# Threshold attention and a gated MLP: thresholding on GpSimd, VectorE or ScalarE by step, and q, k transposes by half tiles

## The chip, the cores and the metric

The kernel runs on one core of a Trainium2 chip. The core has TensorE (PE: matmuls and their weight loads), VectorE (DVE), ScalarE (ACT), GpSimd (POOL) and SyncE (SP, which here issues nearly all DMAs); each has an instruction queue of its own and runs it in order, and waits on the others by semaphores. Matrix products land in PSUM, which DVE and ACT read out; everything else lies in SBUF. The metric is the device time of one execution in microseconds (us), lower is better; the time before is 428.83 us, the median of three runs (428.46 to 429.54).

## The reference

Attention over 8 batches x 8 heads, 576 positions, 64 columns a head, in float32; only scores within tau = 0.02 of a row's maximum take part. Its output, with the heads side by side, goes through a gated MLP that also mixes positions.

```python
scale = 1.0 / np.sqrt(q.shape[-1])                       # 0.125
scores = scale * np.matmul(q, k.transpose(0, 1, 3, 2))
thresh = np.max(scores, axis=-1, keepdims=True) - tau
scores = np.where(scores >= thresh, scores, -1000000000.0)
scores = scores - np.max(scores, axis=-1, keepdims=True)
attn = np.exp(scores)
attn = attn / (np.sum(attn, axis=-1, keepdims=True) + 1e-09)
x = np.matmul(attn, v)          # then (8, 576, 512)
h = np.maximum(x @ w_in, 0.0)   # 1024 columns, halves u and v
v_n = (v - mu) / np.sqrt(var + 1e-06)
v_s = np.einsum('ts,bsd->btd', w_spatial, v_n) + b_spatial[None, :, None]
out = (u * v_s) @ w_out
```

## The kernel before

**Steps.** Heads are taken in pairs, 4 pairs a batch, 32 in all. A pair's 576 rows of queries make 4.5 blocks of 128, so that two pairs make 9 steps, a batch 18 and the kernel 144. A step `g` has 128 query rows against 576 keys for two heads (h = 0, 1). It goes through these stages, each a token in a list:

- `S`, `Y` (`scores`, `scores_end`, line 830): float32 matmuls on 64x64 tiles of the PE array into one of two PSUM rings `s_ring`; heads and row halves run beside each other. Between the first part and the last part of a step lies `G`: an empty instruction on a relay engine (GpSimd, or with a prefix `a` ACT, with `v` DVE), which waits for the first part and for which the last part waits (the two heads share a bank).
- `M` (`top`, line 859): for each head one custom DVE instruction that copies the scores from PSUM to the buffer `e` (a ring of three) and gives the row maximum `peak`, two instructions a step.
- `B` (`shift`, lines 869 on DVE and 873 on GpSimd): `negm`, two numbers a row, from the maxima and tau.
- `E`, `F` (`spread`): one ACT instruction for each head, 128x576, called a half here. A table `WAYS` has a letter for each step. Way `a` (102 steps): Prelu with a slope of 1e30 for negative values (line 890), then `Z` (`exps`, line 925): Exp of both heads at once, 128x1152, to the float16 buffer `p` (a ring of ten). Way `n` (42 steps): Exp straight to float16 (line 887), then on DVE `C` (`keep`, line 909), which makes a mask of bits, and `A` (`pick`, line 918), which ands it with the exponentials as int32 to `p`.
- `T` (line 930): SP issues a DMA that transposes `p` to `pT`; three of 144 steps are transposed on PE instead (`RP`, `rp`).
- `P`, `i`, `p` (lines 505 to 548): PE multiplies `pT` with v and a column of ones, DVE divides by the sum and writes `xn`.

**q and k.** They come by DMA (`ql`, `kl`), are brought into another order on GpSimd (`sq`, line 306, to `qn` and `kn`), and are transposed on PE in float32 by `qk_main`: `QA` four 128x128 transposes of q into one PSUM bank, evicted by `qa` with a factor of 0.125; `QB` and `qb` the same of k without it (lines 448, 422 to 430). The last 64 rows of both go through `QR`, `qr` (line 467), with no factor, which `B`, `E` and `F` make good. PSUM banks for all work but the scores come from a ring of two, `f_ring`.

**The MLP** of one or two batches back runs between the steps: `v` with `ev`, `bv`, `bs`, `ba`, `N` (normalization, the last on GpSimd, lines 696 to 708), `u`, `eu`, `s`, `es`, `o`, `eo`.

**Order.** No scheduler is at work. `ORDER` has a list of some 300 tokens for each of the 8 batches, and `LAST` four short ones for the end; `run_token` issues a token's instructions. A token `X7:1` is stage X of step 7 of the batch one before the list's, `:-1` of the next one. A prefix `d` moves an eviction from ACT to DVE. Each engine's queue has the order in which the tokens stand, and so a token that waits holds up all behind it on its engine.

## Time and profile before

| | before |
|---|---|
| median of 3 runs | 428.83 us (428.46 to 429.54) |
| the profiled execution | 429.39 us |
| its span, first to last instruction | 427.6 us |
| granted TensorE clock | 1.00 |
| packets of the main DMA queue, as a share of 16 engines' span | 102.3% |
| batches, from the first `M` of one to that of the next | 39.4, 48.6, 52.8, 48.3, 49.9, 51.3, 47.6, 46.7 us |
| from the last `M` to the end | 35.5 us |

Rows of the profile are read so: line, engine, operation, what it writes `<-` what it reads, shapes, `x`count, then busy us and mean ns of one; behind the second bar stands the idle time of the engine just ahead of these instructions with what ended it. Rows that a line's or tile's view prints have the shortest, the median and the longest duration in ns instead. PE is matmuls, PEld weight loads. The chain is the work that ended last, followed back from the end. Matmuls overlap and their ends are modelled, so a PE that is busy throughout may still hold small gaps.

### The profile page before, as it was taken

The page shows a single profiled execution, that of the slowest core. Times are in us where ns is not written, and L with a number is a line of the kernel's source. Part 1 is how long each engine was busy: PE and PEld are TensorE (multiplying, and loading weights), DVE is VectorE, ACT ScalarE, POOL GpSimd, SP SyncE. Part 2 cuts the span into 40 slices and gives each one's busy share as a digit, 9 for nine tenths or more (in the row PEclk, how much of TensorE's full clock was granted, in tenths as well). Part 3 has the DMA queues.
Part 4 walks back from the last instruction along what each step waited for, and adds up shares of the span by engine and source line. Part 5 has one row for each costly group of instructions (what it writes and reads, how often), then busy time and mean ns, then how long its engine had stood idle before and what let it go on. Part 6 is the DMA issues. An engine that isn't in the chain of part 4 may idle for free.

```text
span 427.6 us, 13266 instructions
## 1 busy us (share of the span) xinstructions
PE 405.0 (95%) x4978; PEld 253.3 (59%) x5029; DVE 384.0 (90%) x1035; ACT 386.1 (90%) x567; POOL 191.4 (45%) x469
## 2 busy tenths in 40 slices
PE   8778978999999999999999999999999999999995
PEld 4456655566555675575665657656665666565642
DVE  6999989999899899989999999989999989999562
ACT  4999979999999999999999999999999999999362
POOL 2566437763246633554235631374233753255020
PEclk9999999999999999999999999999999999999999
DMA  7999999999999999998999989999989999989913
GB/s 196 288 280 182 263 273 227 168 182 195 239 265 171 214 213 188 204 210 227 214 165 280 211 165 252 217 221 210 236 138 229 228 214 206 160 150 214 180 57 117
DMA packets 224703, 88.18 MB, mean 206 GB/s; under 512 B 195648, under 2 KB 220352, under 8 KB 224640
## 3 DMA queue, kind: packets, MB, share of 16 engines
q1 hardware_dynamic: 224192, 86.75, 102.3%
q8 instruction: 39, 0.64, 0.6%
q10 hardware_dynamic: 368, 0.33, 0.2%
q0 software_dynamic: 80, 0.26, 0.2%
q14 instruction: 24, 0.20, 0.2%
HBM read 32.79 MB, written 9.44 MB: 99 GB/s over the span
## 4 chain that ended last, share of the span: by engine, by line
PE 62%; DVE 11%; ACT 9%; DMA 7%; issue 5%; POOL 3%; SPq 1%; POOLq 0%; DVEq 0%; ACTq 0%
PE s L830 25%; DVE e L859 7%; PE f L752 6%; DMA pT<-p 6%; PE f L448 5%; PE f L510 5%; PE f L723 4%; PE f L656 4%; ACT e L890 3%; PE f L781 3%; ACT e L887 2%; PE f L505 2%; ACT p L925 1%; DMA xT<-xn 1%; PE f L641 1%
## 5 line engine op out<-in xcount | busy, mean ns | idle before, releaser
L859 DVE CUSTOM_DVE_ANT_0 e<-s,zero 128x576 f32<-128x576 f32 x288 | 204.3, 752 | 5.8 <-PE s L830 1.4
L830 PE MATMUL s<-qkT 64*64 64x160 f32 (+1 forms) x2304 | 172.9, 413 | 4.5 <-DVE peak L859 3.7
L890 ACT ACTIVATE e<-e,negm 128x576 f32<-128x576 f32 x204 | 148.3, 766 | 4.8 <-PE s L830 2.3
L830 PEld LDWEIGHTS s<-qkT 64*64 64x64 f32 x2304 | 105.3, 132 | 53.2 <-issue 19.1
L925 ACT ACTIVATE p<-e 128x1152 f16<-128x1152 f32 x102 | 117.1, 1157 | 0.8
L873 POOL TENSOR_SCALAR negm<-peak 128x2 f32<-128x2 f32 x93 | 21.5, 231 | 133.3 <-DVE peak L859 89.7
L887 ACT ACTIVATE e<-e,negm 128x576 f16<-128x576 f32 x84 | 62.4, 767 | 2.0 <-POOL negm L873 1.3
L510 PE MATMUL f<-v,pT 128*128 128x65 bf16 x984 | 44.6, 194 | 0.0
L510 PEld LDWEIGHTS <-pT 128*128 128x128 f16 x1024 | 41.9, 98 | 2.4 <-issue 0.6
L918 DVE TENSOR_TENSOR p<-e 128x576 int32<-128x576 int32 x42 | 34.4, 822 | 0.5
L752 PE MATMUL f<-wsT,vn 128*128 128x512 bf16 x121 | 31.9, 380 | 0.9 <-DVE qkT L424 0.2
L505 PE MATMUL f<-v,pT 128*128 128x130 bf16 x123 | 27.2, 221 | 4.0 <-DMA pT<-p 3.9
L333 POOL CAST v<-vl 128x512 bf16<-128x512 f32 x32 | 21.3, 666 | 18.6 <-PE s L830 17.5
L708 POOL TENSOR_SCALAR vn<-vrel,rs,nm 128x512 bf16<-128x512 f32 (+1 forms) x35 | 27.9, 798 | 3.6
L723 PE MATMUL f<-xT,w_in 128*128 128x512 bf16 x102 | 28.5, 380 | 1.0 <-ACT qkT L430 0.3
L656 PE MATMUL f<-w_in,xT 128*128 128x512 bf16 x98 | 27.0, 380 | 1.4 <-DMA xT<-xn 0.3
L548 DVE TENSOR_TENSOR xn<-f,r 128x384 bf16<-128x384 f32 x46 | 25.2, 554 | 0.7
L781 PE MATMUL f<-w_o,gT 128*128 128x512 bf16 x94 | 25.1, 379 | 0.4
L859 DVE DVE_READ_ACCUMULATOR2_ANT peak<- 128x1 f32 x288 | 23.9, 83 | 0.0
L306 POOL COPY qn<-ql 128x512 f32<-128x512 f32 x31 | 19.7, 636 | 5.9 <-DMA ql<-in_q_dram 2.7
L752 PEld LDWEIGHTS <-vn 128*128 128x128 bf16 x140 | 12.8, 98 | 15.5 <-issue 3.1
L448 PE MATMUL f<-identf,kn 128*128 128x128 f32 x124 | 19.8, 282 | 2.2 <-DVE qkT L424 1.5
(175 smaller groups left out, 560.2 us busy)
## 6 DMA issues: line engine op xcount, KB each, us to landing
vl<-in_v_dram SPq DMA_DIRECT2D x16, 512.0 KB, 5.2
ql<-in_q_dram SPq DMA_DIRECT2D x15, 512.0 KB, 5.5
kl<-in_k_dram SPq DMA_DIRECT2D x15, 512.0 KB, 5.7
out_dram<-oo SPq DMA_DIRECT2D x12, 512.0 KB, 4.2
pT<-p SPq DMA_TRANSPOSE x141, 4.4
uT<-in_moe_w_in_dram SPq DMA_DIRECT2D x3, 512.0 KB, 6.4
uT<-in_moe_w_spatial_dram SPq DMA_DIRECT2D x2, 576.0 KB, 6.8
vx<-in_v_dram SPq DMA_DIRECT2D x16, 64.0 KB, 3.8
```

Source lines behind the costliest of these rows:

```text
L448: nc.tensor.transpose(out=t[:, c * P:(c + 1) * P], in_=nat[i][which][:, c, :], identity=identf)
L505: nc.tensor.matmul(out=t[:, at:at + 130], lhsT=pt[:, 4, rows], rhs=vt[:, 4:6, :].rearrange("p b d -> p (b d)"), start=True, stop=False)
L510: nc.tensor.matmul(out=t[:, at + 65 * h:at + 65 * h + 65], lhsT=pt[:, 5 * h + j, rows], rhs=vt[:, 6 * h + j, :], start=False, stop=(h == 1 ...
L656: nc.tensor.matmul(out=t, lhsT=x_of(b, f, slice(c * P, (c + 1) * P)), rhs=w_in[:, f, 512:1024], start=(f == 0), stop=(f == 3))
L723: nc.tensor.matmul(out=t, lhsT=w_in[:, m, f * P:(f + 1) * P], rhs=x_of(b, m, slice(0, 512)), start=(m == 0), stop=(m == 3))
L752: nc.tensor.matmul(out=t, lhsT=vn[:, c, f * P:(f + 1) * P], rhs=wsT[:, c, 0:512], start=(c == 0), stop=(c == 4))
L781: nc.tensor.matmul(out=t[:n], lhsT=gs[b][:, f, c * P:c * P + n], rhs=w_o[:, f, :], start=(f == 0), stop=(f == 3))
L830: made.append(nc.tensor.matmul(out=s_ring[g % 2][halves[k], at[h] + lo:at[h] + hi], lhsT=qks[n][halves[h], 0, m:m + 64], rhs=qks[n][halves ...
L859: nc.vector.tensor_tensor_reduce(out=e_ring[g % 3][:, h, :], in0=view(s_ring[g % 2], at[h], [[1, S]]), in1=zero.broadcast_to([P, S]), scal ...
L887: nc.scalar.activation(out=half_e(g)[0][:, h, :], in_=s, func=ACT.Exp, bias=bias_, scale=scale if steps[g][1] == 4 else 1.0)
L890: nc.scalar.activation(out=e, in_=s, func=ACT.Prelu, bias=bias_, scale=scale if steps[g][1] == 4 else 1.0, alpha=1e30)
L925: nc.scalar.activation(out=numerators(g), in_=e_ring[g % 3].rearrange("p h s -> p (h s)"), func=ACT.Exp)
```

## The change

**The threshold.** Scores are no longer scaled through q; `M` scales them as it copies (`scale=scale` where 1.0 stood), so that `peak` is scaled too. `B` becomes `bound`: `low` = tau - peak, on GpSimd or with a prefix `d` on DVE. A half (`E`, `F`) becomes one of two things. With a prefix `a` it is a Prelu on ACT as before, then Exp with a bias of -tau. Otherwise it is a `tensor_scalar` on GpSimd, or with `d` on DVE, in place on `e`: add `low`, multiply by 2^-126. What is added lies below tau, so the product is a subnormal number; its bits read as an int32 are the difference in steps of 2^-23, or, where the difference was negative, a number near -2^31. `Z` reads them as int32 with a scale of 2^-23 and a bias of -tau; a negative difference becomes about -256 and its exponential 0. The ways `n`, the mask, the pick and the table `WAYS` go. Of 288 halves 132 are on GpSimd, 60 on DVE and 96 on ACT; `Z` is on ACT for all 144 steps. `e` gets a fourth buffer, `p` loses one of ten.

**q and k.** `QX` makes 16 transposes of 64 rows each, the upper and the lower half of every block in turn, into both PSUM banks of the ring; `qx` and `qy` evict one bank each (q and k of one half). Bringing q and k into order may be done on ACT (`ask`, `asq`), which 27 of 62 are.

**Lists.** All lists are new.

```diff
-    "S0:0 aG0:0 Y0:0 S1:0 G1:0 Y1:0 L7:0 L8:0 M0:0 B0:0 L9:0 Ci1:0 QA1:0 qa1:0 F0:0 M1:0 sk1:0 B1:0 sv0:0 "
+    "S0:0 vG0:0 Y0:0 M0:0 B0:0 ask1:0 L5:-1 S1:0 vG1:0 Y1:0 S2:0 G2:0 Y2:0 M1:0 F0:0 QX1:0 qx1:0 L7:0 L4:-1 "
...
-    e_ring = [const.tile([P, 2, S], F32, name=f"e{i}") for i in range(3)]
-    p_ring = [const.tile([P, 1152], F16, name=f"p{i}") for i in range(10)]
+    e_ring = [const.tile([P, 2, S], F32, name=f"e{i}") for i in range(NE)]
+    p_ring = [const.tile([P, 1152], F16, name=f"p{i}") for i in range(NP)]
...
-    def qk_main(i, which):
-        hold = {}
+    def qk_main(i):
+
+        hold = []
 
         def mm():
-            t = hold["t"] = bank()
-            for c in range(4):
-                nc.tensor.transpose(out=t[:, c * P:(c + 1) * P], in_=nat[i][which][:, c, :],
-                                    identity=identf)
-
-        def ev():
-            if which == 0:
-                evict(qk_of(i)[:, 0, 64:S], hold["t"], mul=scale)
-            else:
-                evict(qk_of(i)[:, 1, 64:S], hold["t"])
-        return "act", mm, ev
+            hold.extend(bank() for _ in range(2))
+            for c in range(8):
+                w, n = divmod(c, 4)
+                for r in range(2):
+                    nc.tensor.transpose(
+                        out=hold[r][:, 64 * c:64 * c + 64], in_=nat[i][w][halves[r], n, :],
+                        identity=identf[halves[r], halves[r]])
+
+        def ev(r):
+            dst = qk_of(i)[:, :, 64:S].rearrange("p w (c s) -> p w c s", c=4)
+            evict(dst[:, :, :, 64 * r:64 * r + 64],
+                  hold[r].rearrange("p (w c s) -> p w c s", w=2, c=4))
+        return "act", mm, lambda: ev(0), lambda: ev(1)
...
+    def bound(g):
+
+        low[g] = small.tile([P, 2], F32, name="low")
+        (nc.vector if on_vector[0] else nc.gpsimd).tensor_scalar(
+            out=low[g], in0=peak[g], scalar1=-1.0, scalar2=tau, op0=ALU.mult, op1=ALU.add)
+
+    def spread(g, h):
+
+        e = e_ring[g % NE][:, h, :]
+        if on_scalar[0]:
+            plain.add(g)
+            nc.scalar.activation(out=e, in_=e, func=ACT.Prelu, bias=low[g][:, h:h + 1], alpha=1e30)
         else:
...
+            (nc.vector if on_vector[0] else nc.gpsimd).tensor_scalar(
+                out=e, in0=e, scalar1=low[g][:, h:h + 1], scalar2=2.0 ** (SHIFT - 149),
+                op0=ALU.add, op1=ALU.mult)
...
+    def exps(g):
+
+        e = e_ring[g % NE].rearrange("p h s -> p (h s)")
+        if g in plain:
+            nc.scalar.activation(out=numerators(g), in_=e, func=ACT.Exp, bias=wrap)
         else:
...
+            nc.scalar.activation(out=numerators(g), in_=e.bitcast(I32), func=ACT.Exp, bias=wrap,
+                                 scale=2.0 ** -SHIFT)
```

`NE` is 4, `NP` is 9, `SHIFT` is 23 for this tau, `wrap` is -tau in every row.

How the queues move is seen at three places, all in batch 0. First PE, where pair 1's q and k are transposed between scores (`s_96`, `s_97` are the score rings, `f_91`, `f_92` the two banks, `rl` the last rows); before:

```order
L448 MATMUL f_91<-identf,qn 128x128 x4
L830 MATMUL s_96<-qkT 64x160 x2
L830 MATMUL s_96<-qkT 64x416 x4
L830 MATMUL s_96<-qkT 64x160 x2
L448 MATMUL f_92<-identf,kn 128x128 x4
L467 MATMUL f_91<-identf,rl_144 128x128
```

and now, from the last couple of the 16 transposes on:

```order
L445 MATMUL f_91<-identf,kn 128x64
L445 MATMUL f_92<-identf,kn 128x64
L815 MATMUL s_97<-qkT 64x160 x2
L815 MATMUL s_97<-qkT 64x416 x4
L815 MATMUL s_97<-qkT 64x160 x2
L464 MATMUL f_91<-identf,rl_143 128x128
```

Two groups on one bank each, with a step of scores between them, have become one group that alternates between both banks. Second ACT, early in batch 0 (`e_...` are the ring's buffers, `p_...` the numerators); before, from the first pair's evictions on:

```order
L430 COPY qkT<-f_92 128x512
L430 COPY qkT<-f_91 128x2x64
L925 ACTIVATE p_111<-e_108 128x1152
L887 ACTIVATE e_109<-e_109,negm 128x576 x2
L890 ACTIVATE e_107<-e_107,negm 128x576 x2
L887 ACTIVATE e_108<-e_108,negm 128x576
L925 ACTIVATE p_113<-e_107 128x1152
L887 ACTIVATE e_108<-e_108,negm 128x576
```

and now:

```order
L422 COPY qkT<-f_91 128x2x4x64
L875 ACTIVATE p_110<-e_106,wrap 128x1152
L859 ACTIVATE e_107<-e_107,low 128x576 x2
L875 ACTIVATE p_112<-e_108,wrap 128x1152
L422 COPY qkT<-f_92 128x2x64
L859 ACTIVATE e_106<-e_106,low 128x576 x2
L873 ACTIVATE p_111<-e_107,wrap 128x1152
L299 COPY kn<-kl_141 128x512
```

Every step had two halves on ACT; now some steps (line 875) leave it only the exponential, and copies of q and k have come. Third GpSimd at about the same place (`v`, `w_in` and `wsb` are v and weights brought to bfloat16); before:

```order
L873 TENSOR_SCALAR negm<-peak 128x2
L333 CAST v_133<-vl_140 128x2x4x64
L339 CAST v_133<-vx_146 64x64 x2
L873 TENSOR_SCALAR negm<-peak 128x2
L333 CAST v_134<-vl_143 128x2x4x64
L339 CAST v_134<-vx_146 64x64 x2
L353 CAST w_in<-uT 128x1024
```

and now:

```order
L861 TENSOR_SCALAR e_108<-e_108,low 128x576
L851 TENSOR_SCALAR low<-peak 128x2
L861 TENSOR_SCALAR e_107<-e_107,low 128x576
L346 CAST w_in<-gT 128x1024
L457 COPY qkT<-qkT 64x64
L861 TENSOR_SCALAR e_107<-e_107,low 128x576
L346 CAST w_in<-uT 128x1024
L861 TENSOR_SCALAR e_106<-e_106,low 128x576
```

The halves stand between the bounds, the casts of the weights and the copies of the first rows (`qkT<-qkT`), and what follows a half in this queue starts after it.

More of the change, by code (lines that the diff above doesn't have):

```diff
@@ L13 @@
 I32 = mybir.dt.int32
-U16 = mybir.dt.uint16
 AX = mybir.AxisListType
@@ L434 @@
     rest_late = (0, 1, 2)
+    halves = [slice(64 * k, 64 * k + 64) for k in range(2)]
     def qk_of(i):
@@ L494, in first @@
         turn(tq, 0, 0, 0)
-        nc.scalar.mul(out=qkt[:, 0, 64:192], in_=tq[:, 0:P], mul=scale)
+        nc.scalar.copy(out=qkt[:, 0, 64:192], in_=tq[:, 0:P])
         for c in range(1, 4):
             turn(tm, P * (c - 1), 0, c)
-        nc.scalar.mul(out=qkt[:, 0, 192:576], in_=tm[:, 0:384], mul=scale)
-    halves = [slice(64 * k, 64 * k + 64) for k in range(2)]
+        nc.scalar.copy(out=qkt[:, 0, 192:576], in_=tm[:, 0:384])
     def weigh(t, at, pt, vt, rows=slice(0, P)):
@@ L850, in scores_end, with top @@
         follow(part(g, 1, 0, S - cut)[0], turned[g])
-    negm, peak = {}, {}
-    def top(g, heads=slice(0, 2)):
-        if g not in peak:
-            peak[g] = small.tile([P, 2], F32, name="peak")
-        for h in range(heads.start, heads.stop):
+    peak, low, plain = {}, {}, set()
+    def top(g):
+        peak[g] = small.tile([P, 2], F32, name="peak")
+        for h in range(2):
             nc.vector.tensor_tensor_reduce(
-                out=e_ring[g % 3][:, h, :], in0=view(s_ring[g % 2], at[h], [[1, S]]),
-                in1=zero.broadcast_to([P, S]), scale=1.0, scalar=float("-inf"),
+                out=e_ring[g % NE][:, h, :], in0=view(s_ring[g % 2], at[h], [[1, S]]),
+                in1=zero.broadcast_to([P, S]), scale=scale, scalar=float("-inf"),
@@ L862, in top @@
                 op0=ALU.add, op1=ALU.max, accum_out=peak[g][:, h:h + 1])
-    def shift(g, engine):
-        nm = negm[g] = small.tile([P, 2], F32, name="negm")
-        down = -(scale if steps[g][1] == 4 else 1.0)
-        if engine is nc.vector:
-            engine.scalar_tensor_tensor(out=nm, in0=peak[g], scalar=down,
-                                        in1=raised[:, 0 if way(g) == "a" else 1, :],
-                                        op0=ALU.mult, op1=ALU.add)
-        else:
-            engine.tensor_scalar(out=nm, in0=peak[g], scalar1=down,
-                                 scalar2=float(tau) + (0.0 if way(g) == "a" else half_step),
-                                 op0=ALU.mult, op1=ALU.add)
@@ L877, in half_e @@
-    def half_e(g):
-        t = e_ring[g % 3].bitcast(F16)
-        return t[:, :, 0:S], t[:, :, S:2 * S]
-    def spread(g, h):
-        s = e_ring[g % 3][:, h, :]
-        e, bias_ = e_ring[g % 3][:, h, :], negm[g][:, h:h + 1]
-        if way(g) in "nrs":
-            nc.scalar.activation(out=half_e(g)[0][:, h, :], in_=s, func=ACT.Exp,
-                                 bias=bias_, scale=scale if steps[g][1] == 4 else 1.0)
-        elif on_act(g):
-            nc.scalar.activation(out=e, in_=s, func=ACT.Prelu, bias=bias_,
-                                 scale=scale if steps[g][1] == 4 else 1.0, alpha=1e30)
-        else:
-            nc.scalar.activation(out=e, in_=s, func=ACT.Exp, bias=bias_)
@@ L1123, in run_token @@
         kind = name.rstrip("0123456789")
-        a = [int(x) for x in name[len(kind):]] if kind not in "SGYMHKBEFZWCAT" else []
-        g = 18 * b + int(name[len(kind):]) if kind in "SGYMHKBEFZWCAT" else 0
+        a = [int(x) for x in name[len(kind):]] if kind not in "SGYMBEFZT" else []
+        g = 18 * b + int(name[len(kind):]) if kind in "SGYMBEFZT" else 0
         if b >= B or g >= len(steps):
-            return
-        if kind in stepwise and way(g) not in stepwise[kind]:
             return
@@ L1185 @@
         nc.vector.memset(zero, 0.0)
-        nc.gpsimd.memset(raised[:, 0], float(tau))
-        nc.gpsimd.memset(raised[:, 1], float(tau) + half_step)
-        nc.vector.memset(ntau, -float(tau))
+        nc.vector.memset(wrap, -float(tau))
         nc.vector.memset(mhalf, -0.5)
-        nc.scalar.activation(out=ctau, in_=ntau, func=ACT.Exp)
+        nc.scalar.activation(out=used, in_=wrap, func=ACT.Exp)
         nc.vector.tensor_copy(out=identb, in_=identf)
```

94 lines of the change are left out of this document (30 added, 64 removed), and 279 rows, old and new, of tables (LAST, ORDER).

## The prediction

> **What bounds the kernel now.** I read the page first, busy shares and then the chain that ended last, and after it the same quantities cut at the batch borders.
>
> ```profile
> PE 405.0 (95%) x4978; PEld 253.3 (59%) x5029; DVE 384.0 (90%) x1035; ACT 386.1 (90%) x567; POOL 191.4 (45%) x469
> ...
> PE 62%; DVE 11%; ACT 9%; DMA 7%; issue 5%; POOL 3%; SPq 1%; POOLq 0%; DVEq 0%; ACTq 0%
> ```
>
> Three engines are at 90% or more and GpSimd is at 45%; the chain is mostly PE, yet over a third of it is not. An average cannot say where that third lies. The borders of the next view are the starts of the first maxima (line 859) of batches 0, 1 and 2, and the end of the last one. Columns: the stretch, its length, then busy time (and instructions) of PE, weight loads, DVE, ACT and POOL.
>
> ```profile
> 7.50:46.90 39.40, 33.29 (x449) 22.29 (x442) 38.66 (x105) 37.02 (x53) 22.21 (x53) 1.00 1.15 257
> 46.90:95.50 48.60, 44.17 (x580) 27.14 (x584) 45.49 (x123) 44.28 (x66) 29.56 (x69) 1.00 1.10 216
> 95.50:392.10 296.60, 291.41 (x3610) 183.65 (x3649) 276.95 (x739) 284.97 (x414) 133.52 (x329) 1.00 1.08 208
> 392.10:427.60 35.50, 30.08 (x312) 16.89 (x314) 18.86 (x49) 17.20 (x32) 4.53 (x9) 1.00 0.55 131
> ```
>
> Batch 0 is bound by DVE (38.66 of 39.40 us) with ACT just behind, and PE idles 6.1 us. In batch 1 all three are within 1.4 us of each other and PE idles 4.4 us. Batches 2 to 7 are PE's: 291.4 of 296.6 us, 5.2 us idle. The tail is the last batch's second half, which has hardly any threshold work. The chain, asked for separately in the first 88 us and in the 297 us after them, agrees:
>
> ```profile
> by line: DVE e L859 17.5%; PE s L830 11.9%; issue 10.9%; ACT e L890 7.0%; DMA pT<-p 6.6%; ACT e L887 6.5%; ACT p L925 4.4%; POOL v L333 3.3%; PE f L723 3.2%; PE f L510 2.9%; POOL v L339 2.5%; DVE p L918 2.4%; POOL w_in L353 1.9%; PE f L448
> ...
> by line: PE s L830 32.4%; PE f L752 8.2%; PE f L448 7.1%; PE f L510 5.8%; PE f L656 5.1%; PE f L723 4.7%; DMA pT<-p 4.6%; PE f L781 4.5%; DVE e L859 4.3%; issue 3.7%; ACT e L890 2.5%; PE f L505 2.0%; DMA xT<-xn 1.7%; ACT e L887 1.2%; PE f L
> ```
>
> So what the change does for ACT and DVE can pay in the first two batches, and from batch 2 on only through PE's own work. Line 448, the q and k transposes that the change rewrites, is 7.1% of the second stretch's chain.
>
> **The threshold: what each engine loses and gets.** The prices stand in these rows.
>
> ```profile
> L890 ACT ACTIVATE e<-e,negm 128x576 f32<-128x576 f32 x204 | 148.3, 766 | 4.8 <-PE s L830 2.3
> L925 ACT ACTIVATE p<-e 128x1152 f16<-128x1152 f32 x102 | 117.1, 1157 | 0.8
> L887 ACT ACTIVATE e<-e,negm 128x576 f16<-128x576 f32 x84 | 62.4, 767 | 2.0 <-POOL negm L873 1.3
> L918 DVE TENSOR_TENSOR p<-e 128x576 int32<-128x576 int32 x42 | 34.4, 822 | 0.5
> L909 DVE TENSOR_SCALAR e<-e 128x1152 uint16<-128x1152 f16 x42 | 19.8, 474 | 1.3 <-ACT e L887 0.9
> L306 POOL COPY qn<-ql 128x512 f32<-128x512 f32 x31 | 19.7, 636 | 5.9 <-DMA ql<-in_q_dram 2.7 <-PE s L830 1.9
> ...
> L428 ACT ACTIVATE qkT<-f 128x512 f32<-128x512 f32 x18 | 10.6, 589 | 3.4 <-PE f L448 3.4
> L869 DVE SCALAR_TENSOR_TENSOR negm<-peak,raised 128x2 f32<-128x2 f32 x51 | 10.3, 202 | 1.3 <-PE s L830 0.6
> ```
>
> ACT loses 148.3 + 62.4 + 117.1 = 327.8 us. It gets 96 Prelu halves at 0.766 (73.5), 144 exponentials over both heads at 1.157 (166.6; 96 of them read the bits as int32, for which no ACT row exists: I price them like the float32 ones, the nearest row, between nothing and a doubling of 1.157) and 27 q and k copies taken from GpSimd, at 0.589 (15.9). That is 386 - 328 + 256 = 314 us.
>
> DVE loses mask and pick, 34.4 + 19.8, and 51 shifts, 10.3. It gets 56 bounds of two numbers (0.2 each, 11) and 60 threshold halves, a form that the trace lacks. Bounds for a half are the plain float32 copy and the two-scalar operation below, stretched from 512 to 576 columns: 0.48 and 0.62 us. I take 0.55, so 33 us. DVE comes to about 384 - 65 + 44 = 363.
>
> GpSimd gets 132 halves and gives up 27 copies of 0.636 (17). The nearest row is its own two-operation TENSOR_SCALAR, 0.767 for 512 columns against 0.192 for 2: 1.13 ns a column, so 0.84 us for 576. From below the copy's 0.610 gives 0.66; from above a doubling, 1.68, which is what a held copy shows (1.204 against 0.610). I take 0.84: 111 us, and POOL comes to 191 + 111 - 17 = 285.
>
> ```profile
> L321 DVE COPY kn<-kl x1: 427/427/427, 3.4 to 3.4; 128x512 f32<-128x512 f32 x1
> L970 DVE TENSOR_SCALAR vn<-vrel,rstd,shift x2: 547/742/936, 412.4 to 413.1; 128x512 bf16<-128x512 f32 x2
> L970 POOL TENSOR_SCALAR vn<-vrel,rstd,shift x1: 768/768/768, 413.0 to 413.0; 128x512 bf16<-128x512 f32 x1
> L708 POOL TENSOR_SCALAR vn<-vrel,rs,nm x35: 761/767/1202, 77.3 to 389.4; 128x512 bf16<-128x512 f32 x28, 64x512 bf16<-64x512 f32 x7
> L873 POOL TENSOR_SCALAR negm<-peak x93: 190/192/719, 9.0 to 393.0; 128x2 f32<-128x2 f32 x93
> L306 POOL COPY kn<-kl x31: 606/610/1204, 9.3 to 358.2; 128x512 f32<-128x512 f32 x31
> L918 DVE TENSOR_TENSOR p<-e x42: 725/758/1476, 12.1 to 395.7; 128x576 int32<-128x576 int32 x42
> ```
>
> These rows also show DVE and GpSimd holding each other up: the same DVE operation takes 547 ns, and 936 when GpSimd's 768 ns one starts just before it; the pick doubles from 758 to 1476, GpSimd's copy from 610 to 1204. [...] What the rows make of it: GpSimd busy 285 of 428 us is two thirds, so about 40 of the 60 DVE halves wait half of 0.84, 17 us on DVE; in return the 84 masks and picks, which do the same now, are gone. DVE ends at 380 at worst, no more than today, so the sum stands without it; it feeds the second rival.
>
> Behind a GpSimd half queue now the bounds, the casts of v and 46 of the 144 relay nops for which PE's last score part waits (68 before; 98 are on ACT and DVE instead of 76). A nop behind a half is late by up to 0.84 us. What covers this is that PE has other work placed between a step's first and last score parts; a fourth e buffer gives every step one more step of time. Each is worth nothing if the cover holds. If a third of the 46 were late by 0.4 it would cost 6 us, and that end stays in the range. One p buffer fewer is covered by the transposes' count and order, which stay at 141 on SP's queue.
>
> **First two batches.** Batch 0 (list 0 puts 15 halves on GpSimd, 10 on ACT, 7 on DVE): DVE loses 7 masks and picks, 7 x 1.296 = 9.1, and gets 7 x 0.55 = 3.9, so 38.66 becomes 33.5, level with PE's 33.3. Batch 1 (21, 6, 9): DVE 45.5 - 5 x 1.296 + 9 x 0.55 = 44.0; POOL 29.6 - 6 x 0.636 + 21 x 0.84 = 43.4; PE 44.2. PE's idle 10.5 us is then the most there is to win. **Batches 2 to 7**: at most PE's 5.2 us. Of the 15.7 us together I take two thirds, 10.5, because GpSimd, loading DMAs and the issue gaps of the chain remain.
>
> **q and k by half tiles.** Before, two groups of four 128x128 transposes a pair; now one group of 16 on 64 rows each, two halves beside each other.
>
> ```profile
> 163.22 0.60 PE L448 MATMUL f<-identf,qn 128*128 128x128 f32 x4
> ...
> L448 PE MATMUL f<-identf,qn 128*128 128x128 f32 x124 | 19.8, 282 | 0.1
> ...
> 209.10 0.48 PEld L830 LDWEIGHTS s<-qkT 64*64 64x64 f32 x16 [0.27 <-issue]
> L830 PEld LDWEIGHTS s<-qkT x2304: 129/133/133, 6.1 to 390.2; 64*64 64x64 f32 x192
> ```
>
> Four transposes take 0.60 us with one at 0.28, so they follow each other every 0.11 us: 8 x 0.11 = 0.87 us a pair. The score rows, the only ones on 64-row tiles, show four tiles loading at once (16 loads of 0.133 in 0.48 us). Two halves should thus run side by side; the streamed columns halve, from 128 to 64, but each half still loads 128 weight columns. If the streamed columns decide, a couple takes 0.055 us and the group 0.44; if the loads decide, 0.11 and 0.87, as now; if halves don't overlap, 16 x 0.11 = 1.74. I take 0.87, no change, because the couple's load is as wide as today's and today's pace of 0.11 would be reached by either. [...] The group needs both f banks at once, so later users of these banks wait for both evictions, 0.59 (ACT) or 0.69 (DVE); scores stand behind nearly every group, and a step of them is over 1 us.
>
> **Sum.** The profiled execution took 429.39 us, 1.8 us more than its span, and the median is 428.83. 429.4 - 10.5 + 0 = 418.9, and 0.6 less against the median: **418 us**.
>
> **Rivals.** (1) *Half tiles at the pace of their streamed columns*: 31 groups save 0.43 us, 24 of them where PE is the bound, 10.3 us: 408. For it: line 448's 7.1% of the chain, and that loads overlap on 64-row tiles. Against it: the width of the load. [...] (2) *GpSimd becomes the pace*, the slower side. Its place is batches 0 and 1, where GpSimd also shapes v and the weights. In batch 1 it holds 25.7 us besides 21 halves, so it decides from (48.6 - 25.7) / 21 = 1.09 us a half. At a mean of 1.4 batch 1 takes 25.7 + 29.4 = 55 us and batch 0 (four copies fewer) 22.2 - 2.5 + 21.0 = 40.7, together 7.7 us more, with nothing won later: 437. For it: held GpSimd operations double, and subnormal results have no row. Against it: most DVE work, the maxima of line 859, holds nothing up. (3) *Halves in series*: 24 x 0.87 = 21 us more, 439. (4) *Waits change places*: SP's transposes (DMA is 7% of the chain, unchanged in number) and late relays eat what is won: 428.5.
>
> **Chances.** Forecast 0.46, (1) 0.24, (2) 0.12, (3) 0.06, (4) 0.12. The forecast's own range is 413 to 424, from all of the 15.7 us to a third of it. The whole range, 404 to 433, takes in (1) and (4) and leaves out (3), most of (2) and the far end of (1), under 0.2. A difference of 0.3% is about what can be told from no change, so faster means under 427.5 and slower over 430.1. Faster: 0.46 + 0.24 + 0.05 of (4) = 0.75; same: 0.07; slower: 0.18.
>
> **What would show it.** Right: batch 0 near 35 us with no engine over 95%; PE still at 98% from batch 2 on; ACT near 315 to 325 in all, POOL near 285, a GpSimd half at 0.8 to 0.9. First rival: a group of 16 lasting 0.6 us or less from first start to last end, and fewer busy PE us in the long stretch. Second: GpSimd halves over 1.1 us on average and DVE or ACT waiting for POOL in the first 95 us. Wrong altogether: PE under 95% busy in batches 2 to 7 with waits for relays or for f banks at its head.

## The result and the profile after

| | before | after |
|---|---|---|
| median of 20 runs each, side by side | 430.25 us (427.26 to 433.24) | 428.61 us (423.57 to 434.78) |
| ratio | | 0.9935, 95% interval 0.9906 to 0.9964 |
| the profiled execution, its span | 429.39, 427.6 us | 428.80, 426.9 us |
| granted TensorE clock of it | 1.000 | 0.991 |
| batches 0 and 1; 2 to 7; the rest, from the profile | 88.0; 296.6; 43.0 us | 88.0; 295.6; 43.3 us |

The change makes the kernel faster by 0.65%, a quarter of the 2.5% that were forecast; on the 428.83 us from which the prediction counts, that is 426.0. The ratio is below that of the medians because it leaves disturbed runs out, five of the 20 of the changed kernel, each over 1.5% above its fastest. A second comparison (the unaltered kernel among the experiments) gave 0.9902 (0.9873 to 0.9931).

The page of the changed kernel, its busy shares and its chain, against the two lines that the prediction began with:

```profile
PE 398.4 (93%) x5230; PEld 248.3 (58%) x5277; DVE 363.0 (85%) x1001; ACT 342.4 (80%) x459; POOL 265.6 (62%) x567
...
PE 71%; DVE 14%; DMA 5%; issue 4%; ACT 3%; SPq 1%; POOL 1%; DVEq 0%; ACTq 0%; POOLq 0%
```

ACT fell from 90% to 80% and DVE from 90% to 85%, as meant, and GpSimd rose from 45% to 62%. No engine but PE is near its limit, yet the span is the same. The stretches between the same borders (length, then busy time of PE, weight loads, DVE, ACT and POOL, the granted clock, the share of the DMA engines, GB/s):

```profile
8.10:47.20 39.10, 31.28 (x446) 20.45 (x439) 34.76 (x95) 31.74 (x40) 29.15 (x58) 0.96 1.15 255
47.20:96.10 48.90, 44.55 (x634) 29.34 (x637) 43.26 (x119) 41.43 (x56) 35.66 (x74) 0.97 1.11 217
96.10:391.70 295.60, 285.65 (x3814) 177.78 (x3846) 262.71 (x718) 249.46 (x329) 194.02 (x421) 1.00 1.06 209
391.70:426.90 35.20, 30.21 (x313) 16.92 (x314) 18.22 (x50) 17.12 (x30) 5.28 (x8) 0.98 0.52 127
```

Three things stand here. In batch 0 DVE has 3.9 us less to do and ACT 5.3 less, and the batch is 0.3 us shorter. In the long stretch PE has 5.8 us less to do, and 1.0 arrives. And the clock, 1.00 in every stretch before, is 0.96 and 0.97 in the first two.

The groups of the page that carry the new prices (busy us, mean ns of one; behind the bar the engine's idle time just ahead):

```profile
L843 DVE CUSTOM_DVE_ANT_0 e<-s,zero 128x576 f32<-128x576 f32 x288 | 203.9, 751 | 17.4 <-PE s L815 14.9
...
L875 ACT ACTIVATE p<-e,wrap 128x1152 f16<-128x1152 int32 x96 | 119.3, 1252 | 7.1 <-POOL e L861 3.3
L861 POOL TENSOR_SCALAR e<-e,low 128x576 f32<-128x576 f32 x132 | 100.2, 759 | 35.9 <-DVE low L851 15.1
L859 ACT ACTIVATE e<-e,low 128x576 f32<-128x576 f32 x96 | 70.5, 767 | 8.3 <-DVE low L851 3.4
L873 ACT ACTIVATE p<-e,wrap 128x1152 f16<-128x1152 f32 x48 | 59.7, 1253 | 1.5 <-PE s L815 0.6
...
L861 DVE TENSOR_SCALAR e<-e,low 128x576 f32<-128x576 f32 x60 | 36.5, 624 | 1.1 <-POOL low L851 0.8
```

and the maxima in the kernel before:

```profile
L859 DVE CUSTOM_DVE_ANT_0 e<-s,zero 128x576 f32<-128x576 f32 x288 | 204.3, 752 | 5.8 <-PE s L830 1.4
```

A GpSimd half takes 0.759 us (0.84 forecast), a DVE half 0.624 (0.55), an exponential 1.25 where 1.157 was forecast, whether it reads float32 or int32. The maxima show where much of DVE's relief of 21 us went: they now wait 14.9 us for PE's scores, where they waited 1.4 us before.

### The profile page after: what moved, and what is told of

The parts are those of the page before. It is cut to its first block, busy times and chain, and to the rows that moved or that the text cites. A ratio compares the mean times of both kernels' runs of the same rounds, so it can differ in the third digit from the quotient of the medians.

```text
span 426.9 us, 13687 instructions
## 1 busy us (share of the span) xinstructions
PE 398.4 (93%) x5230; PEld 248.3 (58%) x5277; DVE 363.0 (85%) x1001; ACT 342.4 (80%) x459; POOL 265.6 (62%) x567
## 4 chain that ended last, share of the span: by engine, by line
PE 71%; DVE 14%; DMA 5%; issue 4%; ACT 3%; SPq 1%; POOL 1%; DVEq 0%; ACTq 0%; POOLq 0%
PE s L815 30%; DVE e L843 8%; PE f L747 7%; PE f L651 5%; PE f L718 5%; PE f L505 5%; PE f L445 4%; DMA pT<-p 3%; PE f L776 3%; DVE e L861 2%; PE f L500 2%; PE f L636 1%; PE f L464 1%; DMA kl<-in_k_dram 1%; DVE qkT L416 1%
## 5 line engine op out<-in xcount | busy, mean ns | idle before, releaser
L843 DVE CUSTOM_DVE_ANT_0 e<-s,zero 128x576 f32<-128x576 f32 x288 | 203.9, 751 | 17.4 <-PE s L815 14.9
L815 PE MATMUL s<-qkT 64*64 64x160 f32 (+1 forms) x2304 | 176.7, 417 | 8.2 <-DVE peak L843 7.1
L875 ACT ACTIVATE p<-e,wrap 128x1152 f16<-128x1152 int32 x96 | 119.3, 1252 | 7.1 <-POOL e L861 3.3
L861 POOL TENSOR_SCALAR e<-e,low 128x576 f32<-128x576 f32 x132 | 100.2, 759 | 35.9 <-DVE low L851 15.1
L859 ACT ACTIVATE e<-e,low 128x576 f32<-128x576 f32 x96 | 70.5, 767 | 8.3 <-DVE low L851 3.4
L873 ACT ACTIVATE p<-e,wrap 128x1152 f16<-128x1152 f32 x48 | 59.7, 1253 | 1.5 <-PE s L815 0.6
L851 POOL TENSOR_SCALAR low<-peak 128x2 f32<-128x2 f32 x88 | 18.6, 211 | 53.5 <-DVE peak L843 28.3
L422 ACT COPY qkT<-f 128x512 f32<-128x512 f32 (+1 forms) x57 | 26.2, 479 | 20.9 <-PE f L445 15.8
L861 DVE TENSOR_SCALAR e<-e,low 128x576 f32<-128x576 f32 x60 | 36.5, 624 | 1.1 <-POOL low L851 0.8
L416 DVE COPY qkT<-f 128x512 f32<-128x512 f32 (+1 forms) x36 | 19.2, 540 | 8.5 <-PE f L445 5.5
L761 DVE TENSOR_TENSOR gT<-f,uT 128x512 bf16<-128x512 f32 x27 | 18.3, 686 | 5.5 <-PE f L747 5.4
```

The source lines that it names most:

```text
L815: made.append(nc.tensor.matmul(out=s_ring[g % 2][halves[k], at[h] + lo:at[h] + hi], lhsT=qks[n][halves[h], 0, m:m + 64], rhs=qks[n][halves ...
L843: nc.vector.tensor_tensor_reduce(out=e_ring[g % NE][:, h, :], in0=view(s_ring[g % 2], at[h], [[1, S]]), in1=zero.broadcast_to([P, S]), sca ...
L859: nc.scalar.activation(out=e, in_=e, func=ACT.Prelu, bias=low[g][:, h:h + 1], alpha=1e30)
L861: (nc.vector if on_vector[0] else nc.gpsimd).tensor_scalar(out=e, in0=e, scalar1=low[g][:, h:h + 1], scalar2=2.0 ** (SHIFT - 149), op0=ALU ...
L873: nc.scalar.activation(out=numerators(g), in_=e, func=ACT.Exp, bias=wrap)
L875: nc.scalar.activation(out=numerators(g), in_=e.bitcast(I32), func=ACT.Exp, bias=wrap, scale=2.0 ** -SHIFT)
```

## The experiments

Each ratio is to the kernel before on the same chip, with its 95% interval.

### Half tiles undone

```diff
-                for r in range(2):
-                    nc.tensor.transpose(
-                        out=hold[r][:, 64 * c:64 * c + 64], in_=nat[i][w][halves[r], n, :],
-                        identity=identf[halves[r], halves[r]])
+                nc.tensor.transpose(out=hold[w][:, n * P:(n + 1) * P], in_=nat[i][w][:, n, :],
+                                    identity=identf)
...
-            evict(dst[:, :, :, 64 * r:64 * r + 64],
-                  hold[r].rearrange("p (w c s) -> p w c s", w=2, c=4))
+            evict(qk_of(i)[:, r, 64:S], hold[r])
```

> The changed kernel (428.61 us, 0.9935 of the one before) with q and k transposed as eight whole 128x128 blocks a pair instead of 16 half blocks, at the same places of the lists, still one group on both PSUM banks; evictions keep their number and size. In the trace of the changed kernel a group of 16 halves holds PE for 0.645 us until the next matmul, two groups of four whole blocks held it for 2 x 0.53 before, so a pair should cost PE 0.3 to 0.4 us more here, 31 pairs 9 to 13. Theory A, the gain of the half tiles is real and was eaten by something else: PE is the bound from batch 2 on, the time rises by 7 to 12 us, ratio to before 1.010 to 1.022. Theory B, after the change PE no longer sets the pace (order and waits do), so what PE saves or loses hardly counts: ratio within 0.990 to 1.000.

Measured: 429.71 us, 0.9986 (0.9957 to 1.0015). The three stretches of its profile:

```profile
8.10:47.10 39.00, 31.20 (x414) 20.40 (x407) 35.40 (x95) 31.78 (x40) 29.31 (x58) 1.00 1.17 257
47.10:93.70 46.60, 44.62 (x604) 29.26 (x607) 43.91 (x118) 41.26 (x56) 35.93 (x74) 1.00 1.07 226
93.70:391.20 297.50, 292.25 (x3627) 182.96 (x3662) 264.03 (x718) 249.34 (x329) 194.16 (x421) 1.00 1.01 208
```

The ratio lies within theory B's range. But it says more: without the half tiles, the new threshold, the fourth `e` buffer and the new lists together cannot be told from no change. Batches 0 and 1 are 2.4 us shorter than before, the long stretch 0.9 longer. The gain that the prediction counted on is not there, and what gain the change has comes with the half tiles, which the prediction had at nothing. Theory B's reason, that PE's saving hardly counts, does not follow: this interval and that of the changed kernel just overlap, so the runs up to here leave open how much the half tiles give. The last pair of experiments measures it.

### The exponential without its bias

```diff
-            nc.scalar.activation(out=numerators(g), in_=e, func=ACT.Exp, bias=wrap)
+            nc.scalar.activation(out=numerators(g), in_=e, func=ACT.Exp)
```

and the same for the int32 form.

> The changed kernel without the bias operand of the exponential (all 144 of them). What is left out: the numerators come out larger by the common factor exp(tau), which the division by their sum takes away again. In the trace of the changed kernel an exponential over both heads takes 1.252 us with the bias, in the kernel before 1.157 without it, so ACT should get 144 x 0.095 = 13.7 us shorter (342 to 328). Theory A, the lateness of ACT's queue (evictions and numerators) is what ate the gain: the time falls by 3 to 8 us, ratio 0.975 to 0.986. Theory B, ACT at 80% is not on the path: ratio 0.990 to 0.996, within 1 us of the changed kernel.

Measured: 427.25 us, 0.9928 (0.9890 to 0.9965). The two groups of its page:

```profile
L875 ACT ACTIVATE p<-e 128x1152 f16<-128x1152 int32 x96 | 110.3, 1160 | 9.3 <-POOL e L861 3.0
...
L873 ACT ACTIVATE p<-e 128x1152 f16<-128x1152 f32 x48 | 55.3, 1160 | 1.7 <-PE s L815 1.0
```

The bias cost 0.092 us an instruction (1.252 against 1.160 us), and int32 costs nothing over float32 (1.160 us for either). Thirteen us taken off ACT change nothing that can be measured: theory B.

### No halves at all

```diff
         if on_scalar[0]:
             plain.add(g)
+            return
...
         else:
+            return
...
-        if g in plain:
+        if True:
```

> The changed kernel with all 288 threshold halves left out (132 on GpSimd, 60 on DVE, 96 on ACT), the bounds kept, and the exponential taken of the scaled scores themselves: no threshold is applied. This is the floor that PE, the transposes by DMA and the order of the lists set. ACT loses 70, DVE 37, GpSimd 100 us. Theory A, the halves and the queues behind them (late relays, late numerators) ate the gain: the time falls to 405 to 415, ratio 0.943 to 0.967. Theory B, something else bounds it (PE with its switches of tile size, the two PSUM banks, the granted clock): 420 to 426, ratio 0.978 to 0.992. The granted clock is to be read too: if it is 1.00 here, the idle stretches of PE that bring it down come from the halves.

Measured: 422.52 us, 0.9838 (0.9799 to 0.9876), granted clock 0.993 to 1.000.

```profile
7.50:43.70 36.20, 29.71 (x446) 19.72 (x439) 30.51 (x88) 24.98 (x30) 15.74 (x41) 1.00 1.12 261
43.70:91.60 47.90, 42.86 (x634) 27.89 (x637) 37.63 (x108) 37.21 (x50) 20.21 (x57) 1.00 1.16 222
91.60:385.60 294.00, 285.62 (x3815) 177.64 (x3848) 243.44 (x674) 194.69 (x249) 118.16 (x326) 1.00 1.07 213
```

This bounds every theory about late halves, late relays and busy queues: with all 288 halves gone the long stretch is at 294.0 us, as with them (295.6 here, 294.0 without the bias), although GpSimd is at 40% there. Batches 0 and 1 gain 3.9 us, and the clock is 1.00 in all three stretches, 0.998 as the mean of its runs, against 0.993 in the runs behind the changed kernel's ratio. The halves are not alone in that, since the version with whole tiles has them all and a mean of 0.997. Theory B. The whole way from the kernel before to one without any half, half tiles included, is 1.6%, or 7 us; the forecast had taken 10.5 out of the relief alone.

### DVE's halves on GpSimd

All 60 tokens `dE`, `dF` become `E`, `F`.

> The changed kernel with the 60 halves of DVE on GpSimd as well (192 in all), at the same places of the lists. [...] Theory A, DVE's queue (maxima waiting behind halves and held copies) is what keeps batches 0 and 1 at 39 and 49 us: the time falls by 2 to 5, ratio 0.982 to 0.990. Theory B, GpSimd's queue with the relays behind its halves sets the pace: the time rises by 3 to 10, ratio 1.000 to 1.017.

Measured: 463.14 us, 1.0762 (1.0727 to 1.0797). Theory B, and far beyond its range. What ACT waited for most, in this kernel:

```profile
ACT p L875 <- POOL e L861: 37.4, 20, 6.3
```

In the changed kernel the same wait was 3.3 us in 6 times. The engines in the chain that ended last:

```profile
PE 61%; POOL 18%; DVE 8%; issue 7%; ACT 4%; DMA 1%; POOLq 0%; DVEq 0%; ACTq 0%
```

GpSimd has 18% of it, where it had 1%, although it is busy for only 302 of 460 us, so no share of busy time announces it. By the lists, the two halves of many steps now stand one behind the other on one engine, behind bounds that wait for DVE, instead of beside each other on two; that this order alone costs the 32 us is argued, since no run changes it alone. GpSimd can set the pace, as in the second rival, but not by long halves: they take 0.745 us here.

### Filling PE's waits

A token of its own ahead of the scores of five steps of batch 0:

```diff
+        if name[0] == "D":
+            for _ in range(int(name[1:]) if it == 0 else 0):
+                nc.tensor.matmul(out=f_ring[(in_turn[0] + 1) % 2].rearrange("p (a b) -> p a b", a=4), lhsT=warm,
+                                 rhs=warm.unsqueeze(1).broadcast_to([P, 4, P]), start=True, stop=True)
+            return
```

What led to it are four windows of the changed kernel, placed where the records of the granted clock change (the same columns as above; the clock is the third number from the end):

```profile
16.17:19.58 3.41, 1.30 (x20) 0.84 (x24) 2.31 (x7) 2.96 (x5) 2.98 (x7) 1.00 1.03 391
19.58:23.00 3.42, 3.42 (x38) 2.34 (x42) 1.73 (x5) 3.23 (x5) 2.40 (x5) 0.50 1.25 188
74.20:77.61 3.41, 1.71 (x27) 1.14 (x23) 3.01 (x8) 3.02 (x7) 2.72 (x9) 1.00 1.64 206
77.61:81.02 3.41, 3.41 (x27) 2.31 (x29) 2.42 (x6) 3.41 (x4) 1.78 (x4) 0.50 1.05 212
```

PE was busy for 1.30 and 1.71 of 3.41 us, and for the next 3.41 us it ran at half its clock. The two low stretches begin 58.03 us apart, 17 times 3.413.

> The changed kernel once more, unaltered, as the measure for the three others on the same chip. Both theories expect its ratio to before within the interval that it had, 0.9906 to 0.9964, and a mean granted clock near 0.991 against 0.996 for the kernel before.

> The changed kernel with 20 matmuls more in batch 0, 128x512 in bfloat16 with a result that nobody reads, into the PSUM bank that is used next: 3 ahead of the scores of step 6, 7 ahead of step 8, 4 ahead of step 10, 3 each ahead of steps 13 and 15, where PE waited 0.7, 1.7, 1.0, 0.8 and 0.7 us for the maxima. They take 20 x 0.21 = 4.3 us of PE, which lie in these waits. Theory A, stretches in which PE is busy for less than half of 3.41 us make the granted clock fall to a half for the next 3.41 us, and this is what the changed kernel loses against the one before: the mean clock rises from 0.991 to 0.994 or more, no half clock between 10 and 50 us in the profile, and the time falls by 1 to 2 us although PE does more (0.997 of the unaltered kernel or less). Theory B, the lower clock has another cause, or it falls where PE has slack and costs nothing: clock as before, time the same or up to 2 us longer.

Measured: the unaltered kernel 425.34 us, 0.9902 (0.9873 to 0.9931), mean clock of its runs 0.995; with the filling 424.88 us, 0.9889 (0.9852 to 0.9925), mean clock 0.997. Their batches 0, first the unaltered one:

```profile
7.80:48.00 40.20, 32.50 (x447) 21.08 (x440) 34.50 (x96) 31.67 (x40) 29.46 (x58) 0.92 1.12 251
```

and with the filling:

```profile
8.00:46.80 38.80, 34.66 (x468) 21.22 (x461) 35.18 (x96) 31.68 (x40) 29.40 (x58) 1.00 1.16 256
46.80:94.00 47.20, 43.25 (x637) 28.18 (x636) 43.44 (x119) 41.57 (x56) 36.41 (x74) 1.00 1.11 215
94.00:386.90 292.90, 287.96 (x3853) 177.98 (x3846) 262.90 (x718) 249.65 (x329) 194.55 (x421) 1.00 1.05 213
```

In these two profiles theory A holds: PE does 2 us more in batch 0, the clock stays at 1.00 and the batch is 1.4 us shorter. Over all runs it is not shown: the difference of 0.5 us lies well inside both intervals. The expectation for the unaltered kernel missed on both counts: its clock was 0.995 and not near 0.991, and its ratio came out just below the interval of the first comparison, so there was little for the filling to win.

### Half of each maximum

```diff
-                out=e_ring[g % NE][:, h, :], in0=view(s_ring[g % 2], at[h], [[1, S]]),
-                in1=zero.broadcast_to([P, S]), scale=scale, scalar=float("-inf"),
+                out=e_ring[g % NE][:, h, 0:288], in0=view(s_ring[g % 2], at[h], [[1, 288]]),
+                in1=zero.broadcast_to([P, 288]), scale=scale, scalar=float("-inf"),
```

> The changed kernel with maxima and copies of the scores over 288 of the 576 columns; the other 288 columns of the e buffers are left as they are, and Prelu has a slope of 1 instead of 1e30. What is left out: half of the columns take no part in the maximum and are not copied. DVE gets 288 x 0.3 = 86 us shorter; threshold halves, exponentials and PE stay as they are. Theory A, batches 0 and 1 are set by the maxima between two PSUM rings (PE waits for them, they wait for PE), which the change left alone: the two batches together fall from 88 to 78 to 82 us, PE is their bound, and batches 2 to 7, where PE is the bound already, change by under 3 us; 414 to 421 in all. Theory B, batches 0 and 1 are set by what arrives (loads and transposes by DMA, the shaping of weights on GpSimd): they stay within 84 to 88 us, and the time within 422 to 428.

Measured: 423.64 us, 0.9856 (0.9826 to 0.9886). The other columns of `e` are cleared first, so batch 0 begins 3 us later.

```profile
10.80:47.10 36.30, 32.33 (x450) 21.27 (x443) 24.82 (x96) 30.64 (x39) 28.55 (x57) 0.95 1.15 260
47.10:93.10 46.00, 42.51 (x637) 27.94 (x636) 33.15 (x119) 41.33 (x56) 36.37 (x74) 1.00 1.09 216
```

Batches 0 and 1 take 82.3 us, just above theory A's 78 to 82, and PE still idles 7.5 us; the time as a whole lies in theory B's 422 to 428, with the later start in it. Seventy-four us less on DVE bought 4 to 5 us in the two batches, against the 86.0 with the filling and the 87.4 without. Not all of it need be DVE's: a batch that starts 3 us later may find more of its loads landed, which was not measured.

### Both, and then without the weights' loads

The edits of the last two reliefs together:

> Both reductions at once: no threshold halves and maxima over 288 columns. What is left out: all thresholding, and half of the columns in the maximum and the copy. Without halves batches 0 and 1 took 36.2 + 47.9 = 84.1 us, with half the maxima 36.2 + 46.0 = 82.2, unaltered 40.2 + 47.3 = 87.5 (86.0 where no half clock fell). Theory A, DVE and the halves bound them one after the other, so that the reliefs add up: 76 to 79 us, near PE's busy 75. Theory B, neither is the bound, and loads, transposes by DMA and PE's own waits at borders remain: 81 to 83. Both expect batches 2 to 7 at 291 to 294, PE's.

Measured: 420.56 us, 0.9762 (0.9727 to 0.9796).

```profile
10.70:42.70 32.00, 29.16 (x446) 19.72 (x439) 20.23 (x88) 24.15 (x29) 13.64 (x37) 1.00 1.13 262
42.70:92.70 50.00, 42.93 (x637) 28.04 (x637) 27.31 (x109) 37.17 (x50) 22.73 (x62) 1.00 1.16 216
```

82.0 us: theory B. Batch 0 gives 4 us more, and batch 1 takes them back. What PE waited for most in these two batches (us, times, longest):

```profile
PE f L500 <- DMA pT<-p: 3.6, 2, 2.5
```

So the same kernel once more, with the weights not loaded:

```diff
-        nc.sync.dma_start(out=wsl[f % 3].rearrange("p c s -> p (c s)")[:, 0:1024],
-                          in_=moe_w_in[f * P:(f + 1) * P, :])
+        nc.gpsimd.memset(wsl[f % 3].rearrange("p c s -> p (c s)")[:, 0:1024], 0.01)
```

and so for `w_spatial` and `w_out`.

> No threshold halves, maxima over 288 columns, and besides that the weights of the MLP are not loaded (w_in, w_spatial and w_out, some 4.4 MB in batches 0 and 1; GpSimd fills their buffers with a constant instead). What is left out: all thresholding, half of the columns in the maximum, the weights' values. With the loads batches 0 and 1 took 32.0 + 49.9 = 81.9 us, and two transposes of p by DMA there stood in the chain with 8.4 and 6.3 us from issue to landing, where 4.4 is the median of all 141. Theory A, the last bound in these two batches is the queue of transposes behind the weights' loads: the landing times fall to 4 to 5 us and the two batches to 76 to 79 us, PE's busy time being 72. Theory B, it is not: 81 to 83.

Measured: 418.53 us, 0.9708 (0.9647 to 0.9768).

```profile
9.60:42.40 32.80, 30.56 (x449) 20.72 (x442) 20.14 (x88) 24.04 (x29) 20.45 (x48) 0.97 1.07 215
42.40:88.00 45.60, 42.16 (x634) 28.00 (x636) 27.43 (x109) 36.98 (x50) 22.99 (x59) 1.00 1.08 198
```

78.4 us, and PE's wait for `pT` is gone from the list of these two batches: theory A by their time. Its mechanism is only half right: from issue to landing a transpose took 2.8 / 4.8 / 7.4 us (shortest, median, longest before 95 us) against 3.0 / 5.1 / 8.4 with the loads. They also start earlier: SP issued the 20th transpose at 66.0 us instead of 72.5, while batch 0 began only 1.1 us earlier. What that is worth to the kernel is another matter. The long stretch with the loads, then without them, and what PE waited for most in the whole execution without them (line 498 there is line 500 above):

```profile
92.70:384.00 291.30, 287.17 (x3854) 177.10 (x3845) 183.78 (x676) 194.21 (x249) 117.69 (x325) 1.00 1.09 215
```

```profile
88.00:384.10 296.10, 285.64 (x3814) 178.12 (x3845) 184.12 (x676) 194.26 (x249) 119.82 (x328) 0.99 1.05 207
```

```profile
PE f L498 <- DMA pT<-p: 4.7, 2, 2.8
```

Both waits lie in the long stretch now, which is 4.8 us longer, and the spans of the two profiled executions are 419.2 and 419.0 us. In these executions the gain of the first two batches does not reach the end; the intervals of the two ratios overlap.

### A version with the waits filled, and the half tiles alone

Filling, no bias, and pair 3's evictions in the second list ahead of a half and a maximum:

```diff
-    "k1:1 aF9:0 qx3:0 T1:0 L1:-1 T5:0 T2:0 L4:-1 T3:0 T7:0 T8:0 T6:0 aE9:0 M11:0 dqy3:0 M12:0 bs3:1 v0:1 "
+    "k1:1 qx3:0 aF9:0 T1:0 L1:-1 T5:0 T2:0 L4:-1 T3:0 T7:0 T8:0 T6:0 dqy3:0 aE9:0 M11:0 M12:0 bs3:1 v0:1 "
```

The place is that of the second low clock. In the changed kernel's timeline (start, us, what; in brackets idle time and what ended it):

```profile
74.87 0.41 PE L445 MATMUL f<-identf,kn 64*128 64x64 f32 x8
...
75.28 0.75 DVE L843 CUSTOM_DVE_ANT_0 e<-s,zero 128x576 f32<-128x576 f32 x1
...
75.64 0.76 ACT L859 ACTIVATE e<-e,low 128x576 f32<-128x576 f32 x1
...
75.96 0.69 DVE L416 COPY qkT<-f 128x512 f32<-128x512 f32 x1
...
76.31 0.56 ACT L422 COPY qkT<-f 128x512 f32<-128x512 f32 x1
...
76.92 0.38 PE L651 MATMUL f<-w_in,xT 128*128 128x512 bf16 x1 [1.64 <-ACT qkT L422]
```

The group of half tiles holds both PSUM banks; its evictions stand behind a half on ACT and a maximum on DVE; and what follows on PE is not scores, as the prediction had it for nearly every group, but a matmul that needs a bank.

> The changed kernel with the 20 filling matmuls, without the bias operand of the exponentials, and with the evictions of pair 3's q and k in the second list each moved ahead of a half on ACT and of a maximum on DVE, because there the matmul behind the group of half tiles (v of the MLP) waited 1.6 us for a PSUM bank. A version that may beat both. Theory A (clock and the two banks taken at once are what was lost): 421 to 424 us, ratio to before 0.978 to 0.986, mean clock 0.995 or more. Theory B (losses move elsewhere): as the unaltered changed kernel, 0.990 to 0.996.

Measured: 423.93 us, 0.9857 (0.9833 to 0.9882), mean clock 0.998. It touches theory A's range; its interval still overlaps that of the unaltered kernel, 0.9873 to 0.9931. PE's wait at this place went from 1.1 us, in the unaltered kernel of the same comparison, to 1.3: the exchange did nothing there, and the best that can be said is that filling and no bias together may be worth 1 or 2 us.

Two more exchanges (`p00` ahead of `dB14`; `S13` ahead of `v0` and `RP00`), and then the same version with whole tiles:

> The version with filling matmuls, no bias operand and earlier evictions of pair 3 (423.93 us, 0.9857 of the kernel before), with two more exchanges in the lists: in the first, the division of x's first block ahead of a bound on DVE, for which the next group of half tiles waited 1.2 us; in the second, the scores of step 13 ahead of v of the MLP, which waited 1.3 us for a PSUM bank behind such a group. Theory A, the two banks taken at once cost what PE waits there: 1 to 2 us less, 0.981 to 0.984 of before. Theory B, PE's wait moves to the next scores: same, 0.984 to 0.988.

> The version with the further exchanges, with q and k transposed as eight whole blocks a pair. It measures the half tiles alone, with the granted clock held up on both sides by the filling matmuls. Theory A, of the 7.2 us of PE time that 23 groups save in batches 2 to 7 (24.0 against 16.8) some 4.5 reach the end: 1.008 to 1.013 times the version with half tiles. Theory B, the gain of half tiles measured so far was the clock's: within 0.3% of it. Theory C, all of PE's saving arrives once the clock and the waits are out of the way: 1.017 or more.

Measured: 426.10 us, 0.9904 (0.9872 to 0.9936), mean clock 0.993, so no version that keeps the whole computation is shown to beat the changed kernel. Theory B for the exchanges, or worse: PE now waited 2.2 us for the maxima ahead of step 13's scores. With whole tiles 431.51 us, 1.0023 (1.0008 to 1.0039), mean clock 0.997, hence 1.012 times the version with half tiles, or 5.4 us: theory A of the second. The clock was not held up on both sides, as the expectation had it; it was lower with the half tiles, so their gain is not the clock's. The long stretch of the two, first with half tiles:

```profile
96.50:389.60 293.10, 288.04 (x3855) 178.10 (x3848) 262.20 (x716) 240.33 (x329) 193.70 (x421) 1.00 1.04 211
```

then with whole ones:

```profile
95.80:394.40 298.60, 294.82 (x3667) 182.92 (x3660) 263.77 (x718) 240.53 (x329) 193.72 (x422) 1.00 1.05 207
```

PE saves 6.8 us with half tiles, and 5.5 of them arrive. The other profiles agree: with half tiles and everything computed this stretch takes 292.9 to 295.6 us, but for the run with DVE's halves on GpSimd, and with whole ones, the kernel before among them, 296.6 to 298.6. Of all the parts of the change this is the one whose gain is shown.

## Why the prediction was wrong

The sign was right and the whole range, 404 to 433 us, held the time, but the forecast's own range, 413 to 424, did not, and the mechanism failed: the 10.5 us came from a part that gave almost nothing, and the part priced at nothing gave what there is.

- **"Of the 15.7 us together I take two thirds, 10.5": the step that failed.** It took PE's idle time in batches 0 and 1 as what a lighter DVE and ACT would give back. Lighter they are (batch 0: 34.8 and 31.7 us, 33.5 forecast for DVE), and with whole tiles the two batches give 2.4 us, the long stretch none. The reliefs show why: the two batches take 86.0 us with the clock held up, 84.1 without any half, 82.3 with half of each maximum, 82.0 with both, 78.4 without the weights' loads as well. Even with every half gone from all three engines they are only 3.9 us shorter than before the change. And reliefs do not add up: 1.9 and 3.7 us apart, together 4.0. An engine at 98% of a batch was one of several that wait for each other. The sizes of the last three are uncertain, since these versions start batch 0 some 2 to 3 us later; counted from the start of the span, batch 1 ends at 94.0, 91.6, 93.1, 92.7 and 88.0 us. Which wait binds the two batches in the end stays open. PE's idle time is the most that can be won, which the prediction said; that two thirds of it can be had was a choice without a row.
- **Batches 2 to 7 are PE's: right.** No relief of DVE, ACT or GpSimd moved them far (294.0 us without halves, 292.7 with half maxima, 291.3 with both, 296.1 without the loads as well, against 292.9 to 295.6 for the changed kernel with and without filling); with whole tiles on PE they took 297.5 and 298.6. "PE at 98%" came out at 97 (98 in the second profile). Some of what looks idle is missing records: in this stretch the profile of the kernel before has 39 matmuls fewer than weight loads (3610 and 3649), that of the changed kernel 32, its second profile none. So part of the 5.2 us that the prediction took for idle was probably work.
- **Half tiles at 0.87 us a group, "no change": wrong, towards the first rival.** A pair's transposes and what comes next on PE, in the timeline of the changed kernel (start, us, instructions):

```profile
113.29 0.46 PE L445 MATMUL f<-identf,qn 64*128 64x64 f32 x8
113.59 0.41 PE L445 MATMUL f<-identf,kn 64*128 64x64 f32 x8
113.93 0.58 PE L815 MATMUL s<-qkT 64*64 64x160 f32 x6
```

  and in that of the kernel before, where q and k are two groups:

```profile
111.78 0.66 PE L448 MATMUL f<-identf,qn 128*128 128x128 f32 x4
112.27 1.24 PE L752 MATMUL f<-wsT,vn 128*128 128x512 bf16 x4
...
113.86 0.65 PE L448 MATMUL f<-identf,kn 128*128 128x128 f32 x4
114.35 0.39 PE L590 MATMUL f<-identb,xn 128*128 128x128 bf16 x4
```

  This pair holds PE for 0.64 us instead of 2 x 0.49; over the 23 groups of the long stretch the 6.8 us of the last two experiments are 0.3 a pair. From first start to last end it takes 0.71 us, where the prediction's sign for the first rival was 0.6 or less. The old pace was 0.12 us a block, not 0.11, and a couple of halves takes 0.08: less than the 0.11 of the forecast, in which the loads decide, and more than the 0.055 of the first rival. The width of the load, the argument against that rival, did not hold: the recorded loads of the half tiles are as long as those of whole ones (0.138 and 0.140 us against 0.141 in the median), and with two tiles of 64 rows the couples follow each other faster all the same. The rival's own price of 10.3 us was twice what arrived, 5.4.
- **The group's two banks, "scores stand behind nearly every group": the cover was missing at one place,** for 1.6 us, which is quoted above; exchanging tokens there moved the wait to the scores. Ahead of the groups themselves PE waited 3.4 us in all, against 2.2 before. It is a small term.
- **Durations.** GpSimd half 0.759, DVE half 0.624 (just past the upper bound of 0.62): both near. That the two hold each other up shows in the shortest, median and longest duration of a half on either (the view of line 861 in the changed kernel):

```profile
L861 POOL TENSOR_SCALAR e<-e,low x132: 739/745/1072, 10.3 to 394.4; 128x576 f32<-128x576 f32 x132
L861 DVE TENSOR_SCALAR e<-e,low x60: 481/516/1386, 14.4 to 395.2; 128x576 f32<-128x576 f32 x60
```

  On DVE the mean lies 0.108 us above the median, 6.5 us for 60 halves, against 17 at worst in the prediction; DVE is not the bound. With DVE's halves gone from beside them, the longest of 192 halves on GpSimd takes 0.757 us instead of 1.072, beside as many maxima. ACT came to 342 instead of 314 us. About 13 of the 28 are the bias operand of 144 exponentials, which stood in the diff and was not priced; evictions that the new lists give to ACT make some 8 more (57 to 65 us). The sum itself was off by much of the rest: ACT's instructions overlap, its groups add up to 419 us before against 386 of busy time, so taking the groups' 327.8 off the 386 took too much. ACT's 13 us proved to be worth nothing.
- **Late relays** (6 us in the range): without any half in the queues the long stretch stays the same, so they cost nothing there.
- **The clock was no term at all.** In the 15 runs of the changed kernel that the first ratio uses, the mean granted clock was 0.993; seven of them with 0.994 or more averaged 426.1 us, four with 0.990 or less 428.4. The kernel before had 0.995 in 56 runs beside the experiments. At some 3 us for 0.01 (the slope in these 15 runs) the difference is worth about 1 us, and it would fit that the comparison in which the changed kernel's clock was 0.995 gave 0.9902 and not 0.9935. This is a correlation and two profiles; the run that was to prove it moved the time by too little.
- **The rivals.** The second (GpSimd sets the pace) did not come: 0.759 is far from 1.09. Nor did the third: a pair takes 0.64 us and not 1.74. The fourth (waits change places) is what happened to the threshold's gain, though not by late relays: DVE waits for scores, PE for maxima and, in the relieved versions, for transposes by DMA.

In sum: half tiles some 5 us, threshold and lists about none (0.6 us with whole tiles, inside the interval). The two comparisons of the changed kernel gave 2.8 and 4.2 us; about 1 of what is missing may be the clock, and the rest stays open.

## What to carry to other kernels

Idle time of the bounding engine is a ceiling for a gain, not an estimate of it; before a share of it is claimed, ask what the second and the third bound of that stretch are, and a version that leaves the work out altogether answers for the price of one run. Where one engine is at 98% over hundreds of microseconds, only what shortens its own instructions counts, so price those most carefully. And TensorE, when it waits more, may lose its clock besides: here it fell to 0.50 for 3.41 us after PE had been busy for 1.30 and 1.71 of 3.41 us.
